# A spectral gate kernel: the inverse sequence step in 32x32 tiles, one joint last step for both branches

## The chip, the cores and the metric

The kernel runs on one core of one Trainium2 chip. The metric is device microseconds of one execution. Three runs of the kernel before gave 138.37, 138.78 and 139.69 us, with a median of 138.78. One more execution was profiled.

The engines are named as in the profile: PE is TensorE's matmul (PEld its weight load), DVE is VectorE, ACT is ScalarE, POOL is GpSimd and SP is SyncE, which issues most transfers. SPq and POOLq are the queues of transfers that SP and GpSimd issue.

## The reference

```python
B, S, D = 1, 2048, 1024; Df = D // 2 + 1

def ref(x, w_r, w_i):
    X = rfft2(x.astype(float32), axes=(-2, -1))
    X = X * (w_r + 1j * w_i)
    return irfft2(X, s=(S, D), axes=(-2, -1)).astype(bfloat16)

g = sigmoid((A_x * gate_w).sum(-1, keepdims=True))
out = g * ref(A_x, A_w_r, A_w_i) + (1 - g) * ref(A_x, B_w_r, B_w_i)
```

Both branches, A and B, transform the same x (2048 rows of 1024, bf16), so the forward transform is shared. Each branch multiplies it by its own complex weights (2048 x 513) and is transformed back. A gate g, one number per row, mixes the two results.

## The kernel before

A row's number is split as s = 16*p + n2, with p on the 128 partitions and n2 from 0 to 15; a frequency row is split as well. The transforms are matmuls with fixed matrices, in these steps. Every step leaves its result in PSUM, in units of 1,024 f32 per partition (two of the eight banks), and an **eviction** copies each unit to SBUF as bf16, on ACT or on DVE, whichever the plan gives it to (`ev`, line 469; on ACT it is recorded at line 479, on DVE at line 480). All matmuls are recorded at line 454 and all elementwise operations of two operands at line 457.

- **x and S1** (`xrows`, `stage_s1`): the 1,024 columns are folded into sums and differences (`fS`, `fT` on DVE), and 16 units of eight 256-column matmuls do the sequence transform over p. The result Z fills R3.
- **gate** (`gate_row`): matmuls on strips of 32 array columns, 512 wide, reduce Z with the folded gate weights.
- **D** (`stage_d`, 16 groups kg): the transform over d, eight matmuls of 256 columns each; its weights are slices of R3, so R3 is in use until the last D. Result Q.
- **S2** (`stage_s2`): the remaining 16-point step of the sequence transform, with full 128x128 matrices from SK. Result X in R4, shared by both branches. The frequency l=512 is kept apart (`x512`, `p512`, `v512`, `v512_row`).
- **PA, PB** (`prod`): the complex product with the weights of A and B. For two groups at a time DVE does a product of 2,048 elements (`mul`) and a sum of 1,024 (`sum`) for the real part and the same for the imaginary part: 32 products and 32 sums in all.
- **IA, IB** (`stage_i1`): per branch and group, eight matmuls of 256 columns do the inverse 16-point step. Result V, in R1 for A and in R5 for B.
- **EA, EB** (`stage_dinv`): per branch and n2, eight matmuls of 256 columns do the inverse over d: VA into R3, VB into a ring buffer. A Dinv needs all V of its own branch only, so A's can run while B's products are still made.
- **S** (`s1inv`): per n2, four matmuls of 512 columns do the inverse sequence step for both branches and add them in PSUM. The gate is folded into their matrices (`gmix`: RA, RB). DVE then unfolds the columns (`h0`, `h1`, `y0`, `y1`), and SP stores the rows.

The weights come in 28 transfers from SP (`wpart`), half of them in reversed rows of 513 elements (1,026 bytes). A's go to R5, B's to R2, which is free when the matrices F have been used by S1.

The order of the work is computed when the program is built. `Plan.run` is a list scheduler with estimated costs: among the operations that are ready on an engine it takes the one with the lowest rank and gives it an engine and PSUM or ring space. The rank is a line per kind of step from the table `ORDER` (line 18). Each engine then executes its own list in that fixed order, and waits on semaphores.

Of the kernel before, what the change touches and what calls it, by code (L numbers as in the profile page):

```python
# [15 lines left out]
KC = ((0, 4), (4, 8), (8, 16))  # L16
CELL = 512
ORDER = {"in": (0, 0), "x": (48.5, 5.31), "gate": (128.3, 6.12), "D": (35.3, 4.27), "S2": (2.5, 7.29),
         "PA": (46.6, 2.74), "IA": (49.9, 4.36), "x5": (67.7, 12), "row": (123.1, 12), "EA": (124.8, 11.5),
         "PB": (99.2, 5.5), "IB": (130, 4.9), "gm": (54.4, 5.49), "EB": (126.2, 10.71), "S": (130, 12),  # L20
         "U": (0.5, 2.73)}
DEPTH = ((0, 2), (2, 4), (4, 8), (8, 12), (12, 16))
# [8 lines left out]
def make_consts():  # L31
    C = {}
    pi2 = 2 * np.pi
    n1 = np.arange(128)[:, None, None]
    n2 = np.arange(16)[None, :, None]
    kord = np.arange(16)[:, None] + 32 * np.arange(4)[None, :]
    kord[0] = 0, 32, 16, 48
    kord = kord.reshape(-1)
    k1 = kord[None, None, :]
    a = pi2 * ((16 * n1 * k1 + n2 * k1) % 2048) / 2048.0  # L40
    F = np.zeros((128, 16, 64, 2))
    F[..., 0] = np.cos(a)
    F[..., 1] = -np.sin(a)
    F[:, :, 0, 1] = (-1.0) ** np.arange(128)[:, None]
    C["F"] = F.reshape(128, 2048)
    R = np.zeros((64, 2, 16, 128))
    at = a.transpose(2, 1, 0)
    R[:, 0] = np.cos(at) / 2048
    R[:, 1] = np.sin(at) / 2048
    R[0, 1] = ((-1.0) ** np.arange(128))[None, :] / 2048  # L50
    C["RM"] = R.reshape(128, 2048)

    m = np.arange(256)[None, :]
    DM = np.zeros((128, 4, 2, 256))
    for h in range(2):
        d = (h * 128 + np.arange(128))[:, None] + 0.5
        lev, lod = 2 * m, 2 * m + 1
        les = np.where(m == 0, 512, 2 * m)
        DM[:, 0, h] = np.cos(pi2 * lev * d / 1024)
        DM[:, 1, h] = -np.sin(pi2 * lod * d / 1024)  # L60
        DM[:, 2, h] = -np.sin(pi2 * les * d / 1024)
        DM[:, 3, h] = np.cos(pi2 * lod * d / 1024)
# [4 lines left out]
    for par in range(2):  # L67
        for h in range(2):
            l = (2 * (h * 128 + np.arange(128)) + par)[:, None]
            DI[:, par, h, 0] = np.where(l == 0, 1.0, 2.0) / 1024 * np.cos(pi2 * l * d / 1024)  # L70
            li = np.where(l == 0, 512, l)
            DI[:, par, h, 1] = -np.where(li == 512, 1.0, 2.0) / 1024 * np.sin(pi2 * li * d / 1024)
    C["DI"] = DI.reshape(128, 2048)

    S2 = np.zeros((2, 3, 128, 128))
    KI = np.zeros((2, 2, 128, 2, 16, 4, 2))
    for z in range(2):
        for pm in range(2):
            for k2 in range(16):
                for j in range(4):  # L80
                    po = pm * 64 + k2 * 4 + j
                    i, cj, spec = (3 - j if pm else j), pm == 1, False
                    if z == 1:
                        i, cj = ((0, 1, 0, 1), (2, 3, 3, 2))[pm][j], 32 * j + 16 * pm > 64
                        spec = i == 0
                    for q2 in range(16):
                        w = np.exp(-1j * pi2 * q2 * (k2 + cj) / 16)
                        if spec and j == 2:
                            w = w * np.exp(-1j * pi2 * q2 * 64 / 2048)
                        r0, r1 = q2 * 8 + i * 2, q2 * 8 + i * 2 + 1  # L90
                        wr, wi = w.real, w.imag
                        sg = -1.0 if cj else 1.0
                        if spec:
                            r = r1 if j == 2 else r0
                            S2[z, 0, r, po] = wr
                            S2[z, 1, r, po] = wi
                        else:
                            S2[z, 0, r0, po] = wr
                            S2[z, 0, r1, po] = -sg * wi
                            S2[z, 1, r0, po] = wi  # L100
                            S2[z, 1, r1, po] = sg * wr
                        cr, ci = wr, -wi
                        K = KI[z, :, po, :, q2, i, :]
                        if spec:
                            ri = 1 if j == 2 else 0
                            K[0, 0, ri], K[1, 0, ri] = cr, -ci
                            K[0, 1, ri], K[1, 1, ri] = ci, cr
                        else:
                            K[0, 0, 0], K[1, 0, 0] = cr, -ci
                            K[0, 0, 1], K[1, 0, 1] = -sg * ci, -sg * cr  # L110
                            K[0, 1, 0], K[1, 1, 0] = ci, cr
                            K[0, 1, 1], K[1, 1, 1] = sg * cr, -sg * ci
        S2[z, 2] = -S2[z, 1]
    C["SK"] = np.concatenate([S2.transpose(2, 0, 1, 3).reshape(128, 768),
                              KI.reshape(2, 2, 128, 256).transpose(2, 0, 1, 3).reshape(128, 1024)], 1)
    gs = np.full((64, 2), 8.0)
    gs[:, 1] = -8.0
    gs[0] = 4.0
    M = np.zeros((128, 64))
    M[:, :16] = gs.reshape(128, 1)  # L120
    M[::32, 16] = 1.0
    M[:16, 32:48] = np.eye(16)
# [135 lines left out]
class Plan:  # L258
# [28 lines left out]
    def run(self, keys):  # L287
# [18 lines left out]
        dma_free = 0.0  # L306
# [5 lines left out]
        def fit(t):  # L312
# [4 lines left out]
            if a == "ps":  # L317
                spots = range(0, 8, 2) if t.n == 2 else range(7, -1, -1)
            else:
                spots = range(len(c) - t.n + 1)  # L320
# [30 lines left out]
        while done < len(nodes):  # L351
            for e in ("sp", "pool", "pe", "act", "dve"):
                if free[e] > now + 1e-9:
                    continue
                for item in ready[e]:
# [7 lines left out]
                    if n.dma:  # L363
                        dma_free = max(dma_free, now + 1.3) + lat
                        n.end = dma_free + 0.9
# [39 lines left out]
def bass_gated_mix__spectral_gfnet__spectral_gfnet__prompt_kernel(  # L405
# [11 lines left out]
    def ap(t, off, dims, p0=0, np_=128):  # L417
# [4 lines left out]
    R3 = sb("R3", 16384)  # L422
    R4 = sb("R4", 16384)
# [3 lines left out]
    SK = sb("SK", 1792)  # L427
# [3 lines left out]
    NCELL = 26  # L431
    RING = sb("RING", NCELL * CELL)
    V6 = sb("V6", 256)
    X5 = sb("X5", 32)
    P5 = sb("P5", 192)
    V5 = sb("V5", 256)
# [5 lines left out]

    P = Plan({"ps": 8, "ring": NCELL, "late": 32},
             {"ps": ("ps", 4), "p1": ("ps", 8), "st": ("ring", 4), "q": ("ring", 3), "t": ("ring", 2),
              "pp": ("ring", 2), "g": ("ring", 1), "vb": ("ring", 4), "o": ("late", 3), "h": ("late", 2),
              "y": ("late", 3), "w": ("ring", 1)})
# [3 lines left out]
    WR = {0: R5, 1: R2}  # L450
    VR = {0: R1, 1: R5}
# [41 lines left out]

    def cload(eng, t, off, key, a, b, keys, **kw):
        dma("c_" + key, eng, lambda: [(ap(t, off, [[1, b - a]]).bitcast(dt.uint16), cst[key].ap()[:, a:b])],
            (b - a) * 256e-6, 400, [], keys, **kw)
# [16 lines left out]
    cload("sp", SK, 0, "SK", 0, 1792, ["SK"])  # L513

    def wpart(b, ci, pm, c):
# [3 lines left out]
        k0, k1 = KC[ci]  # L519
# [4 lines left out]
        def part(ka, kb, r0, step):  # L524
            o = [[n, kb - ka], [1, n]] if step < 0 else [[1, (kb - ka) * n]]
            i = [[step * n, kb - ka], [1, n]] if step < 0 else [[1, (kb - ka) * n]]
            prs.append((AP(T, 64 * pm * pt + c * NW + ka * NS, [[pt, 64]] + o),
                        AP(src.tensor, src.offset + r0 * n, [[32 * n, 64]] + i)))
        if pm == 0:
            part(k0, k1, k0, 1)  # L530
        else:
            if k0 == 0:
                part(0, 1, 16, 1)
# [265 lines left out]
    for n2 in range(16):  # L799
        stage_dinv(0, n2)  # L800
# [82 lines left out]
```

## Time and profile before

| what | us |
|---|---|
| median of three runs | 138.78 |
| span of the profiled execution, first to last instruction | 137.1 |
| DVE products, 32 of 2,048 elements | 38.1 |
| ACT evictions to R and RING, 105 of 1,024 elements | 74.6 + 32.4 |
| DVE evictions, 23 of 1,024 elements | 23.2 + 5.1 |
| PE matmuls of the inverse over d, 256 of 256 columns | 30.5 |
| PE matmuls of the inverse 16-point step, 256 of 256 columns | 31.0 |
| landing of a 513 KB weight transfer of B, from its issue | 18.5 to 20.2 |

The profiled execution's own whole time is not recorded apart from its span. The span runs from the first to the last instruction and lies 1.7 us below the median of the runs, which also hold what lies around the instructions. In the groups of the page the columns are line, engine, operation, output and input with their shapes and the count, then the busy time with the mean duration of one in ns, then the idle time of the engine just before, with what ended it. In the timeline rows the columns are start, length, engine and operation with the count; consecutive like operations are merged into one row. In the rows of ten engine slices each digit is the busy share of a 40th of the span (3.4 us).

### The profile page before, as it was taken

The numbers are of one execution on the slowest core, as the hardware profiler recorded it, in microseconds if no ns is written. First come the engines' busy times: TensorE is split into PE (matmuls) and PEld (weight loads), VectorE is DVE, ScalarE is ACT, GpSimd is POOL, SyncE is SP. The second block draws the span as 40 slices with busy tenths as digits, with TensorE's granted clock in tenths as the row PEclk, the third lists the DMA queues.
The fourth block names the chain that finished last, engine by engine and source line by source line (L and its number), as shares of the span: only waits on it lengthen the run. The fifth ranks groups of instructions, "written<-read, shape, count | busy, mean of one in ns | idle before, by whom it ended". The sixth has DMA issues, their size and how long they took to land.

```text
span 137.1 us, 2504 instructions
## 1 busy us (share of the span) xinstructions
PE 124.1 (91%) x1034; PEld 91.2 (67%) x1034; DVE 118.8 (87%) x159; ACT 112.7 (82%) x123; POOL 0.2 (0%) x4
## 2 busy tenths in 40 slices
PE   6859999999999949999977999999999999999930
PEld 2348886767778627766745888778887757666500
DVE  0399977389999679999999999999996889998992
ACT  6458886879989976999888799999787689898960
POOL 0000000000000000000000000000000000000000
PEclk9999999999999999999999999999999999999997
DMA  4999999999999999992000000000000021465254
GB/s 128 412 428 426 367 197 196 205 213 169 168 341 201 199 194 225 177 164 42 0 0 0 6 0 0 0 5 0 0 1 5 0 108 45 170 244 203 82 226 153
DMA packets 8269, 19.53 MB, mean 143 GB/s; under 512 B 961, under 2 KB 5057, under 8 KB 7618
## 3 DMA queue, kind: packets, MB, share of 16 engines
q1 hardware_dynamic: 8112, 19.36, 54.4%
q8 instruction: 8, 0.13, 0.5%
q10 hardware_dynamic: 146, 0.02, 0.1%
q14 instruction: 3, 0.02, 0.1%
HBM read 15.17 MB, written 4.19 MB: 141 GB/s over the span
## 4 chain that ended last, share of the span: by engine, by line
PE 53%; DMA 16%; DVE 15%; ACT 7%; SPq 3%; issue 3%; DVEq 0%
PE PS L454 53%; DMA R<-in_B_w_i_dram 13%; DVE RING L457 10%; ACT R L479 6%; DMA R<-in_A_x_dram 4%; SPq L485 3%; DVE R L480 3%; DVE R L457 1%; ACT RING L479 1%; DVE RING L480 1%; DVE P L457 0%; ACT V L479 0%; DVEq L215 0%; DVE X L480 0%
## 5 line engine op out<-in xcount | busy, mean ns | idle before, releaser
L479 ACT ACTIVATE R<-PS 128x1024 bf16<-128x1024 f32 x77 | 74.6, 1062 | 10.8 <-PE PS L454 10.6
L457 DVE TENSOR_TENSOR RING<-R 128x2048 bf16<-128x2048 bf16 (+1 forms) x48 | 48.3, 1046 | 6.8 <-DMA R<-in_A_x_dram 4.7
L479 ACT ACTIVATE RING<-PS 128x1024 bf16<-128x1024 f32 x28 | 32.4, 1180 | 4.0 <-PE PS L454 3.7
L454 PE MATMUL PS<-SK,RING 128*128 128x256 bf16 x256 | 31.0, 273 | 2.5 <-DVE R L480 1.9
L454 PE MATMUL PS<-DI,R 128*128 128x256 bf16 x256 | 30.5, 273 | 0.0
L454 PEld LDWEIGHTS PS<-SK,RING 128*128 128x128 bf16 x256 | 23.7, 98 | 7.5 <-DVE R L480 2.2
L454 PEld LDWEIGHTS PS<-DI,R 128*128 128x128 bf16 x256 | 24.7, 98 | 5.3 <-ACT R L479 0.2
L480 DVE CAST R<-PS 128x1024 bf16<-128x1024 f32 x19 | 23.2, 1223 | 4.4 <-PE PS L454 4.3
L457 DVE TENSOR_TENSOR R<-R 128x1024 bf16<-128x1024 bf16 (+1 forms) x36 | 21.3, 629 | 0.5
L457 DVE TENSOR_TENSOR RING<-RING 128x1024 bf16<-128x1024 bf16 x32 | 21.0, 689 | 0.1
L454 PE MATMUL PS<-RING,SK 128*128 128x511 bf16 (+1 forms) x96 | 16.9, 308 | 0.1
L454 PE MATMUL PS<-R,RING 128*128 128x256 bf16 x128 | 14.5, 273 | 2.0 <-DVE RING L457 1.4
L454 PE MATMUL PS<-DM,R 128*128 128x256 bf16 x128 | 16.1, 272 | 0.0
L454 PEld LDWEIGHTS PS<-R,RING 128*128 128x128 bf16 x128 | 12.3, 98 | 4.6 <-DVE RING L457 1.7
L454 PEld LDWEIGHTS PS<-DM,R 128*128 128x128 bf16 x128 | 11.6, 97 | 2.8 <-DVE R L480 0.4
L454 PEld LDWEIGHTS PS<-RING,SK 128*128 128x128 bf16 x96 | 7.7, 97 | 6.8 <-DVE RING L480 0.3
L454 PE MATMUL PS<-R,FM 128*128 128x512 bf16 x32 | 9.5, 379 | 0.4 <-ACT R L479 0.4
L454 PE MATMUL PS<-RING,DM 128*128 128x512 bf16 x32 | 9.5, 379 | 0.0
L480 DVE CAST RING<-PS 128x1024 bf16<-128x1024 f32 x4 | 5.1, 1264 | 3.0 <-PE PS L454 3.0
L454 PEld LDWEIGHTS PS<-RING,DM 128*128 128x128 bf16 x32 | 3.1, 98 | 3.8
L454 PE MATMUL PS<-RING 128*128 128x512 bf16 x10 | 4.4, 631 | 1.2 <-DVE RING L555 1.2
L454 PEld LDWEIGHTS PS<-R,FM 128*128 128x128 bf16 x32 | 3.0, 98 | 2.3 <-ACT R L479 0.9
(33 smaller groups left out, 27.3 us busy)
## 6 DMA issues: line engine op xcount, KB each, us to landing
out_dram<-R SPq DMA_DIRECT2D x7, 512.0 KB, 2.6
R<-in_A_x_dram SPq DMA_DIRECT2D x3, 1024.0 KB, 9.5
R<-in_A_w_r_dram SPq DMA_DIRECT2D x2, 513.0 KB, 19.0
R<-in_A_w_i_dram SPq DMA_DIRECT2D x2, 513.0 KB, 20.8
R<-in_B_w_r_dram SPq DMA_DIRECT2D x2, 513.0 KB, 18.5
R<-in_B_w_i_dram SPq DMA_DIRECT2D x2, 513.0 KB, 20.2
R<-in_A_x_dram SPq DMA_DIRECT2D x2, 512.0 KB, 4.6
R<-in_A_w_r_dram SPq DMA_DIRECT2D x3, 256.5 KB, 15.9
```

The source lines that it names most:

```text
L454: return lambda e: e.matmul(o, l, r, start=start, stop=stop, skip_group_check=True)
L457: return lambda e: e.tensor_tensor(out=o, in0=a, in1=b, op=op)
L479: return [lambda e: e.activation(o, i, ACT.Copy)]
L480: return [lambda e: e.tensor_copy(o, i)]
L485: lambda e: [lambda q, d=d, s=s: q.dma_start(d, s) for d, s in pairs()],
```

## The change

**The forward 16-point step and the inverse one in 32x32 tiles.** The frequency rows are ordered anew on the partitions (`kap`, `img` in `make_consts`), so that the 16-point steps act within blocks of 32 rows. S2 now has four groups sq. For each, four D (`j` = 0 to 3) give four Q, and two chunks of 32 matmuls of 512 columns follow, each with a 32x32 matrix at its own tile of the array. The Nyquist column l=512 is made by 64 one-column matmuls per group (S25) and one small eviction (X5) and then lies in the rows of X as the first or last of 513 columns; the old separate chain is gone.

**Products summed by TensorE.** `prod` does only the products, four per group sq and branch, each of 4 x 513 elements, into new areas (R2 for A, R5 for B). The sums are done in PSUM: `stage_i1` runs per group sq and part c a chunk of 64 matmuls of 512 columns in 32x32 tiles, four for each of sixteen tiles, into four banks, with two evictions of 1,024.

**Rows turned SBUF to SBUF.** V goes to ring buffers, and per branch and group four transfers of 256 KB (`turn`) move it so that the whole inverse sequence index lies on the partitions (TV: R1 for A, R2 for B). A transfer reads 128 partitions and writes 16 rows of 2 KB into each of 8 partitions. They are issued from GpSimd's queue, except that half of B's are issued by SP.

**One joint sequence step and one inverse over d.** For each n2, S1i is 16 matmuls of 128 columns (both branches added in PSUM, result G), and Di is eight matmuls of 256 columns. `stage_dinv` is gone. S1i reads the turned rows of both branches.

**Weights.** They come in 34 transfers per branch, each with 16 partitions. Those of A for j = 2 and 3 are issued from GpSimd's queue, after x rows 8 have landed. B's now go to R3, after Z has been read by all D and gate matmuls.

**Order.** Rank and, for many evictions, the engine are given per operation in two strings (`RANK`, `ENGS`) instead of the table `ORDER`. The scheduler keeps a separate transfer time line for each issuing queue. x comes in eight transfers instead of five.

```diff
-ORDER = {"in": (0, 0), "x": (48.5, 5.31), "gate": (128.3, 6.12), "D": (35.3, 4.27), "S2": (2.5, 7.29),
...
+WSPLIT = (((0, 4), (4, 16)), ((0, 8), (8, 16)))
+RANK = (
...
+DEPTH = ((0, 2), (2, 4), (4, 6), (6, 8), (8, 10), (10, 12), (12, 14), (14, 16))
...
-                        dma_free = max(dma_free, now + 1.3) + lat
+                        dma_free[e] = max(dma_free.get(e, 0.0), now + 1.3) + lat
...
-    WR = {0: R5, 1: R2}
-    VR = {0: R1, 1: R5}
+    WR = {0: R5, 1: R3}
+    TV = {0: R1, 1: R2}
+    PR = {0: R2, 1: R5}
...
+            prs.append((AP(T, (32 * j + odd) * pt + c * NW + ka * NS, [[2 * pt, 16]] + o),
+                        AP(src.tensor, src.offset + r0 * n, [[128 * n, 16]] + i)))
...
+        g = b == 0 and j > 1
+        dma("W%d%d" % (b, ci), "pool" if g else "sp", lambda: prs, (k1 - k0) * 0.0164, 205, [("x", 8)] if g else [], [("W", b, ci, j, odd, c)],
+            after=[("Z", m) for m in range(16)] if b else [], n=len(prs))
...
-                    f.append(mm(psl(t, o, [[1, 256]]), ap(R3, qq * 2048 + kg * 128, [[1, 128]]),
+                    f.append(mm(psl(t, o, [[1, 256]]), ap(R3, qq * 2048 + j * 512 + sq, [[4, 128]]),
...
-        ev("Q", 1024, lambda: (rg(q, 0, [[512, 2], [1, 2], [2, 256]]), psl(t, 0, [[512, 2], [256, 2], [1, 256]])),
-           [(t,)], [(q, 0, 2)], slow=True, alloc=[q])
+        ev("Q", 1024, lambda: (rg(q, 0, [[8, 2], [16, 64], [1, 8]]), psl(t, 0, [[512, 2], [8, 64], [1, 8]])),
+           [(t,)], [(q, 0, 2)])
...
+                            f.append(mm(psl(x5, (i * 2 + c) * 2 + u, [[1, 1]], 32 * j, 32), ap(SK, o, [[1, 32]]),
+                                        rg(qs[j], 1023 if u else 511, [[1, 1]]), True, True))
...
+                for m in range(2):
+                    for j in range(4):
+                        for i in range(4):
+                            w = z(i, j) + ((0, 2), (1, 0))[c][m] * 32
+                            f.append(mm(psl(t[i // 2], i % 2 * 512, [[1, 512]], 32 * j, 32), ap(SK, w, [[1, 32]], 32 * i, 32),
+                                        rg(qs[j], m * 512, [[16, 32], [1, 8], [8, 2]], 32 * i, 32), m == 0, m == 1))
...
-            P.add("sum", vt(1024), lambda e, t=t, c=c, op=op: [
...
+            w = ap(T, 2 * m * NS + o * NW, [[NS, 2], [(NW, -NW)[o], 2], [1, NS]])
+            P.add("mul", vt(4 * NS), lambda e, o=o, w=w: [tt(rp(b, p, (s0 * 4 + o * 2) * NS, [[4 * NS, 2], [NS, 2], [1, NS]]), x, w, ALU.mult)],
...
+                for pr in range(4):
+                    for j in range(4):
+                        for i in range(4):
+                            w = 192 + (192 if sq == i == j == 0 else 0) + (c * 3 + (0, 1, 2, 2)[pr]) * 32
+                            f.append(mm(psl(t[j // 2], j % 2 * 512, [[1, 512]], 32 * i, 32), ap(SK, w, [[1, 32]], 32 * j, 32),
+                                        rp(b, p, (i * 4 + pr) * NS + c, [[1, 512]], 32 * j, 32), pr == 0, pr == 3))
...
+        for j in (0, 2, 1, 3):
+            dma("turn", "sp" if b and j > 1 else "pool", lambda j=j: [(AP(TV[b], (32 * j + sq) * pit[id(TV[b])], [[4 * pit[id(TV[b])], 8], [1024, 16], [1, 1024]]),
+                                              rg(v[j // 2], j % 2 * 1024, [[1, 1024]]))], 0.262, 215,
...
+    allv = [("V", b, sq, j) for b in range(2) for sq in range(4) for j in range(4)]
...
+                        f.append(mm(psl(t, blk * 128, [[1, 128]]), ap(TV[b], off, [[2, 128]]), ap(rm, n2 * 128, [[1, 128]]), b == 0, b == 1))
...
+            pe("S1i", [128] * 16, fns, allv + [("RA", n2 // 4), ("RB", n2 // 4)], [(t,)], alloc=[t])
...
+            pe("Di", [256] * 8, fns, [(gt, 0, 2), "DI"], [(t,)], alloc=[t])
...
-    P.run(lambda n: ORDER[n.key[0]][0] + ORDER[n.key[0]][1] * n.key[1])
+    P.run(lambda n: int(RANK[2 * n.at:2 * n.at + 2], 36))
```

444 lines of the change are left out of this document (200 added, 244 removed), and 3 rows, old and new, of the table P.

## The prediction

> **What bounds the kernel now.** I read first the page's busy times and slices.
>
> ```profile
> span 137.1 us, 2504 instructions
> PE 124.1 (91%) x1034; PEld 91.2 (67%) x1034; DVE 118.8 (87%) x159; ACT 112.7 (82%) x123; POOL 0.2 (0%) x4
> PE   6859999999999949999977999999999999999930
> DVE  0399977389999679999999999999996889998992
> ACT  6458886879989976999888799999787689898960
> DMA  4999999999999999992000000000000021465254
> GB/s 128 412 428 426 367 197 196 205 213 169 168 341 201 199 194 225 177 164 42 0 0 0 6 0 0 0 5 0 0 1 5 0 108 45 170 244 203 82 226 153
> ```
>
> TensorE has hardly a gap from slice 3 to slice 38, and VectorE and ScalarE stand close behind it. DMA is full for the first 62 us and nearly idle from there to 110: x comes at 412 to 428 GB/s, then both weight sets at about 200. Then a table of busy time by stretch that I cut at the end of the sequence step (22.3), near the end of the first product's work (70), at the first joint output (100) and at the last matmul's end (131.5).
>
> ```profile
> 22.30:70.00 47.70, 45.76 (x397) 32.37 (x396) 42.42 (x50) 42.08 (x43) 0.00 (x0) 1.00 0.91 172
> 70.00:100.00 30.00, 28.26 (x275) 23.73 (x275) 29.95 (x41) 27.07 (x35) 0.00 (x0) 1.00 0.01 1
> 100.00:131.50 31.50, 31.04 (x221) 21.20 (x218) 28.27 (x41) 27.54 (x30) 0.00 (x0) 1.00 0.26 101
> 131.50:137.10 5.60, 0.00 (x0) 0.00 (x0) 2.96 (x8) 1.02 (x1) 0.00 (x0) 0.86 0.48 187
> ```
>
> The columns are PE, PEld, DVE, ACT, POOL, clock, DMA share, GB/s. PE fills every stretch; in 70 to 100 DVE is full too. So a gain needs all three engines relieved. The granted clock is 1.00 up to the tail. Prices come from the page's groups and from timeline rows:
>
> ```profile
> L479 ACT ACTIVATE R<-PS 128x1024 bf16<-128x1024 f32 x77 | 74.6, 1062 | 10.8 <-PE PS L454 10.6
> L457 DVE TENSOR_TENSOR RING<-RING 128x1024 bf16<-128x1024 bf16 x32 | 21.0, 689 | 0.1
> R<-V SPq DMA_DIRECT2D x2, 4.0 KB, 1.7
> 76.50 19.36 ACT L479 ACTIVATE R<-PS 128x1024 bf16<-128x1024 f32 x21 [0.77 <-PE PS L454]
> 68.50 0.61 PE L454 MATMUL PS<-R,G 128*32 128x512 bf16 x8
> 70.34 0.25 PE L454 MATMUL PS<-MS,FM 128*128 128x1 bf16 x4
> 70.77 0.42 PE L454 MATMUL PS<-MS,V 16*16 16x16 bf16 x8 [0.17 <-ACT V L479]
> 94.97 1.06 PE L454 MATMUL PS<-RM,ZG 128*128 128x128 bf16 x16
> 131.50 1.02 ACT L479 ACTIVATE R<-PS 128x1024 bf16<-128x1024 f32 x1 [0.21 <-PE PS L454]
> ```
>
> Durations overlap, so I price by spacing: an ACT eviction 19.36/21 = 0.92 us, a DVE eviction 1.14 (1.22 long; successors start 1.14 later), a 2,048-element product 1.14, a 256-column matmul 0.109 (92 in the full 10 us from 80), a 128-column one (1.06-0.22)/15 = 0.056. Eight gate matmuls of 512 columns on four 32-column strips take 0.61: 0.38 for one, 0.22 until the second four start, so four run side by side and start within some 4 ns of each other.
>
> **The change part by part.**
>
> *Removed.* The 32 sums: 21 us of DVE. Of 128 evictions of 1,024 elements 16 go: Z, Q, X and V stay at 16, 16, 16, 32, but VA+VB+o (48) become G+o (32). 14 Q evictions on ACT cost 1.32 instead of 1.02 (every second element is written); the new Q writes runs of eight, as V does already at 1.02, so I price it as V. On PE: S2 (64 x 0.215 = 13.8), I1 (256 x 0.109 = 27.9), both Dinv (27.9), S1i (13.8), and l=512's own chain with its two row DMAs.
>
> *Added on PE.* S1i is 256 matmuls of 128 columns, 256 x 0.056 = 14.3; one Di is 14.0. S2 is 256 and I1 1,024 matmuls of 32x32 with 512 columns. No row shows tiles in different rows running together. Bounds: all 16 at once, 0.216 per sixteen, gives 3.5 and 13.8; only the four columns at once, as the gate rows show, 0.864 per sixteen, gives 13.8 and 55. I take the first, since the gate rows show the 4 ns starts that it needs and neighbours in the new order lie in different tiles; both ends are kept. S25's 256 one-column matmuls lie between 4 ns (gate) and 35 ns (the 16x16 row: (0.42-0.17)/7), 1 to 9 us; I take 4, as two in a row share a tile. Each change of tiling costs about 0.1 (gate to D starts 0.32 after the last gate group, against 0.22): some 50 changes, 5 us. D's weights at step 4 are priced as I1's step 2, whose loads take 98 ns like unit-step ones; S2's moving operand at inner step 8 is unseen, at worst twice 3.5, and hidden. Between 22.3 and the joint step PE then has D 14 + S25 4 + S2 3.5 + I1 13.8 + gate and gm 3 + 5 = 43.
>
> [...]
>
> *Added on DVE.* Products have 2,052 elements instead of 2,048 in rows of 513. Weight rows of before start at odd offsets already and run at the 1.14 rate, so I add nothing; at worst an odd row length halves the rate, +1.14 x 32 = 36 us.
>
> *Added DMAs.* 32 turns of 256 KB, SBUF to SBUF, in 2 KB pieces: 24 from GpSimd's queue, 8 from SP's. GpSimd issues none before; its bound is an SP issue (0.55) below and an eviction-long 1.1 above, and only the last turns count. Landing: 1.7 (the 4 KB V row) at least, 2.6 (a 512 KB output) at most for one; I take 2.3 plus 0.6 of issue.
>
> [...]
>
> *Moved.* B's weights go to R3, so they wait until every D and gate matmul has read Z; before they followed the sequence step, and the last D runs at 61.8. Their 34 small issues queue on SP behind that wait with only output stores and turns behind them; 34 x 0.6 = 20 us of issue lies beside the transfer. A's weights are split between SP and GpSimd's queue, but the slices show about 200 GB/s at full DMA share for all weights, so splitting gives no more.
>
> *The sum, against the profiled 137.1.* (1) S1 is unchanged: its last matmul is at 22.3. (2) From there to the joint step VectorE and ScalarE have 64 evictions, 32 products (36.5), RA and RB 3.3, sigmoids and gate rows 5.0, X5 0.8. With a evictions on ACT, 0.92a+5.0 = 1.14(64-a)+40.6 gives a = 53 and 53.5 us each: more than PE's 43, so they are the bound. Start-up: four D (3.5), S25 and S2 (2), evictions, so the first product is near 30 as before, with only some eight Q evictions to do: 3 idle each. That ends at 78.8. (3) The joint step needs all rows of both products, a barrier that before has not: last I1 chunk 0.9, eviction 1.1, issue 0.6, landing 2.3: 5, so 83.8. (4) PE does S1i and Di, 28.3 plus 1.2 for the first G: 113.3 (VectorE and ScalarE have 32 evictions and 21 us of folds, 26 each, which fit). (5) The tail after the last matmul stays 5.6: 118.9. (6) Packing: before, PE's spacings between 9.6 and 131.5 add up to 115 of 122, 6% lost; 6% of stages 2 and 4 is 5, giving 123.9. The span lies 1.7 below the median of the runs (138.78), so **125.6**.
>
> Checked from the other side, B's weights: 32 evictions of Q and X, five by DVE before its products, 27 x 0.92 on ACT, put the last D near 47; 4.2 MB at 200 GB/s is 21; half of A's turns (4.2 MB at 428 GB/s, 10) shares the time, 5: 73. Eight products follow (9.1), then 5, 29.5, 5.6 and 1.7: 124. The two agree within 2, so either may be the one that ends last.
>
> **The rivals.**
>
> *B's weights land late (slower).* D spread between the products, as before (last one at 61.8), puts the landing at 61.8+21+5 = 88, and the time at 88+50.9 = 139. From a landing at 75 on, each us comes out at the end; from 88 the change loses. With the turns wholly inside it is 144; I take 142. For it: the wait is new, the slices show full DMA at 200 GB/s. Against: PE has 10 us of slack to run D early.
>
> *Issue binds the small tiles.* If each pair of load and matmul costs 29 ns, as in the row at 70.34 ((0.25-0.16)/3, all on one tile), the 256+1,024 pairs of S2 and I1 cost 37 instead of 17.3: PE's 43 becomes 63 against the others' 56.5, and 125.6 becomes 132. For it that row and the 16x16 one, against it the gate rows.
>
> *The tiles do not run together by rows,* so the change does not do what it says. S2 and I1 cost 69 instead of 17.3; PE has 95 in stage 2 against 56.5: 125.6+38.5 = 164, slower. Nothing for it but the lack of a row. Half-rate products (36 more on DVE, half of it passed to ACT as evictions: 144 to 162) share its chance.
>
> **How the numbers follow.** Forecast 0.55 (117 to 133), late weights 0.20, issue 0.12, serial tiles or half-rate products 0.10, 0.03 for better than 117 (early weights and full packing). The range 117 to 145 leaves out that 0.10, the 0.03 and a little of the late weights. Faster, by over 1% (below 137.4; less can't be told from no change): 0.55 + 0.10 of issue + 0.03 = 0.68. Within: 0.05 from the edges of issue and late weights. Slower: 0.10 + 0.17 = 0.27.
>
> **What would show it.** I1 chunks of 64 matmuls at 0.86 plus a switch (0.1): tiles together; 1.7 is issue, 3.5 serial. DVE and ACT at 95 each, PE below 100. Products at 1.22 long. The last D before 50, B's last weights near 74, the first joint matmul at 84 to 90, 29.5 from it to the last matmul, 5.6 after it. Wrong if products cost over 1.3, turns land later than 4, or a clock below 1.00 follows PE's idle time ahead of the joint step.

## The result, and the profile after

The changed kernel took 169.45 us (median of four runs, 167.99 to 171.67), the kernel before 138.64 beside it: a ratio of 1.2144, 95% interval 1.203 to 1.2257. The ratio leaves out the slowest of the four (171.67), which fell into a slower state. The change is slower; 125.6 was forecast. The profiled execution took 170.03, its span is 168.2.

The page of the changed kernel, its busy times and four of its slice rows (a slice is now 4.2 us):

```profile
span 168.2 us, 4991 instructions
PE 105.5 (63%) x2258; PEld 77.2 (46%) x2258; DVE 93.4 (56%) x116; ACT 97.9 (58%) x109; POOL 22.8 (14%) x44
...
PE   7898980099999975638620004761700599999950
...
PEclk9999999558999999996555555799585599999996
DMA  5999999992000056699999998078767000333635
GB/s 170 417 274 412 271 258 260 272 194 45 4 0 4 8 158 150 146 204 199 205 191 223 177 208 162 4 150 220 203 204 224 9 0 4 125 129 127 248 154 225
```

The work is as small as forecast: DVE 93 and ACT 98 against 95 each. Matmuls (PE) are at 105 of 168, where less than 100 was forecast, part of it at half clock. No engine is full any more. PE, at 9 nearly throughout before, has three holes: near 25 to 34 us, 85 to 103 and 122 to 132. The clock, 0.995 on average before, is 0.830, at 0.5 about those holes. DMA was nearly idle from 62 to 110 before; now it moves some 150 to 220 GB/s from 58 to 130, with one gap near 107, so it is busy in the holes too.

The same by stage: the wait ahead of D, D and S2, the rest up to the first product of B, from there to the joint step, the joint step (columns as in the table by stretch of before):

```profile
22.30:33.97 11.67, 2.49 (x37) 0.93 (x36) 0.69 (x1) 2.73 (x4) 0.00 (x0) 0.79 1.04 258
33.97:57.60 23.63, 23.63 (x408) 17.53 (x408) 14.04 (x16) 18.30 (x22) 0.00 (x0) 0.89 0.23 42
57.60:97.30 39.70, 18.06 (x771) 9.70 (x768) 17.15 (x20) 22.34 (x25) 9.48 (x16) 0.74 0.85 178
97.30:132.10 34.80, 11.88 (x513) 7.53 (x513) 20.77 (x18) 13.26 (x14) 4.74 (x8) 0.70 0.68 164
132.10:162.40 30.30, 29.95 (x384) 27.94 (x384) 23.44 (x33) 24.55 (x26) 0.00 (x0) 0.95 0.24 98
```

The joint step is as priced, and starts 48 us after the 83.8 of the forecast. From 57.6 to 132.1 the engines have work for 38 (DVE) and 36 us (ACT) in 74.5. What they wait for is in the groups and the list of transfers (the last figure there is the median from issue to landing):

```profile
L460 DVE TENSOR_TENSOR R<-R 128x2052 bf16<-128x2052 bf16 (+2 forms) x68 | 58.3, 908 | 22.9 <-DMA R<-in_B_w_r_dram 19.9
L457 PE MATMUL PS<-DM,R 128*128 128x256 bf16 (+1 forms) x256 | 34.2, 264 | 9.2 <-DMA DM<-c_DM 9.2
L457 PE MATMUL PS<-FM,R 128*128 128x128 bf16 x128 | 16.4, 229 | 10.4 <-DMA R<-RING 10.4
...
R<-RING POOLq DMA_DIRECT2D x24, 256.0 KB, 8.8
...
R<-in_B_w_r_dram SPq DMA_DIRECT2D x15, 128.2 KB, 9.9
...
DM<-c_DM SPq DMA_DIRECT2D x1, 512.0 KB, 21.7
```

Three arrivals, one for each hole. DM, the matrices of D, is issued at 12.2 among A's weights and lands at 33.9. B's products wait 19.9 us for B's weights: the last D ran at 57.6, the weights were issued from 57.9 to 94.0 and the last landed at 105.9. The joint step waits 10.4 us for the last turns, issued at 124.7 and 125.3 and landed at 132.1; over the 24 from GpSimd's queue the landing takes 8.8 in the median and up to 14.8. A fourth wait is in the timeline of PE, in I1 of A (the brackets hold the idle time before a row and what ended it; "issue" is time in which the profile shows nothing that was waited for):

```profile
71.63 1.14 PE L457 MATMUL PS<-R,SK 32*32 32x512 bf16 x64 [0.69 <-ACT R L482]
73.46 0.40 PE L457 MATMUL PS<-R,SK 32*32 32x512 bf16 x4 [0.69 <-ACT RING L482]
75.87 2.81 PE L457 MATMUL PS<-R,SK 32*32 32x512 bf16 x124 [2.01 <-issue]
79.11 0.61 PE L457 MATMUL PS<-R,SK 32*32 32x512 bf16 x4 [0.44 <-ACT RING L482]
81.47 3.63 PE L457 MATMUL PS<-R,SK 32*32 32x512 bf16 x124 [1.74 <-issue]
```

The first row is a chunk of 64 small matmuls in 1.14 us, so the sixteen tiles do run together. But twice PE stops after four matmuls and goes on 1.7 to 2.0 us later, after 128 pairs of load and matmul. During each stop the trace has a packet of 16 KB on the queue that the page lists as instruction (73.6 to 74.6 and 79.3 to 80.2).

### The profile page after: what moved, and what is told of

Read it like the earlier page. It is cut to its first block, busy times and chain, and to the rows that moved or that the text cites. A ratio compares the mean times of both kernels' runs of the same rounds, so it can differ in the third digit from the quotient of the medians.

```text
span 168.2 us, 4991 instructions
## 1 busy us (share of the span) xinstructions
PE 105.5 (63%) x2258; PEld 77.2 (46%) x2258; DVE 93.4 (56%) x116; ACT 97.9 (58%) x109; POOL 22.8 (14%) x44
## 4 chain that ended last, share of the span: by engine, by line
DMA 29%; SPq 25%; PE 25%; DVE 10%; ACT 5%; issue 3%; POOL 0%; DVEq 0%
SPq L488 25%; PE PS L457 25%; DMA DM<-c_DM 13%; DMA R<-RING 10%; DVE R L460 9%; DMA R<-in_B_w_r_dram 6%; ACT RING L482 5%; DVE RING L483 1%; ACT R L482 1%; POOL R L488 0%; DVEq L221 0%
## 5 line engine op out<-in xcount | busy, mean ns | idle before, releaser
L482 ACT ACTIVATE RING<-PS 128x1024 bf16<-128x1024 f32 x58 | 56.4, 1037 | 54.1 <-PE PS L457 52.5
L460 DVE TENSOR_TENSOR R<-R 128x2052 bf16<-128x2052 bf16 (+2 forms) x68 | 58.3, 908 | 22.9 <-DMA R<-in_B_w_r_dram 19.9
L457 PE MATMUL PS<-R,SK 32*32 32x512 bf16 x1024 | 24.2, 480 | 32.7 <-DVE R L460 21.9
L457 PE MATMUL PS<-DM,R 128*128 128x256 bf16 (+1 forms) x256 | 34.2, 264 | 9.2 <-DMA DM<-c_DM 9.2
L482 ACT ACTIVATE R<-PS 128x1024 bf16<-128x1024 f32 (+2 forms) x38 | 35.5, 987 | 7.7 <-PE PS L457 7.6
L457 PEld LDWEIGHTS PS<-R,SK 32*32 32x32 bf16 x1024 | 14.8, 92 | 42.8 <-DVE R L460 24.3
L457 PEld LDWEIGHTS PS<-DM,R 128*128 128x128 bf16 x256 | 27.3, 111 | 12.3 <-DMA DM<-c_DM 9.3
L457 PE MATMUL PS<-FM,R 128*128 128x128 bf16 x128 | 16.4, 229 | 10.4 <-DMA R<-RING 10.4
L483 DVE CAST R<-PS 128x1024 bf16<-128x1024 f32 (+2 forms) x14 | 14.8, 1071 | 3.6 <-PE PS L457 3.6
L457 PE MATMUL PS<-DI,RING 128*128 128x256 bf16 x128 | 15.2, 273 | 0.3 <-ACT RING L482 0.3
```

What stands on the lines that cost most here:

```text
L457: return lambda e: e.matmul(o, l, r, start=start, stop=stop, skip_group_check=True)
L460: return lambda e: e.tensor_tensor(out=o, in0=a, in1=b, op=op)
L482: return [lambda e: e.activation(o, i, ACT.Copy)]
L483: return [lambda e: e.tensor_copy(o, i)]
```

## The experiments

Three theories. **1**: late arrivals; DM, B's weights and the turns follow each other on one set of DMA engines. **2**: TensorE's small tiles, their instructions and the half clock. **3**: a turn is slow by its own form. "Joint" is the start of the joint step (132.1 in the changed kernel). The edits change `P.order`, the finished order, behind `P.run`, except where other lines are shown. Times are of one run each with a profile, except in the one run whose interval is given; the kernel before took 138.7 to 140.4 beside them. The changed kernel's own four runs lie 3.7 us apart, so a difference of one or two us between single runs says little.

### The order of the loads

```diff
+    early = [n for n in P.order if n.name in ("c_DM", "c_SK")]
+    rest = [n for n in P.order if n not in early]
+    k = 1 + max(i for i, n in enumerate(rest) if n.name == "x" and n.eng == "sp")
+    P.order = rest[:k] + early + rest[k:]
```

> Only the loads of DM and SK move: they are issued by SP right after the last x load instead of among A's weights; every engine's order is otherwise that of the changed kernel. Theory 1 (a chain of late arrivals, because the weights on two queues share one set of DMA engines): D starts at 23 to 25 instead of 33.97, the last D ends near 47 instead of 57.8, B's weights are issued from there, and the whole time falls by about the same 10 us, to 157 to 163. Theory 2 (small tiles at the pace of issue hold TensorE): D starts earlier, but the time stays within 4 of 170. Theory 3 (the turns set the end by their own slowness): at most 5 of the 10 arrive at the end, 165 to 168.

164.4 us, between the ranges of theories 1 and 3 and outside that of theory 2. D starts at 25.8 instead of 34.0, and the last one runs at 52.2; 5.6 of the 8.2 us come out at the end, against the profiled run's 170.0. Next, with it, B's weights in two halves, the first one first:

```diff
+    wb = iter(sorted((n for n in P.order if n.name in ("W10", "W11")), key=lambda n: n.name))
+    P.order = [next(wb) if n.name in ("W10", "W11") else n for n in P.order]
```

> The load of the D matrices goes ahead of A's weights (as in the first experiment, 164.4 us), and of B's weights the first half (frequency rows k2 0 to 7, all that the first four product groups need) is issued before the second half; nothing is left out. Theory 1 (a chain of late arrivals): the first product of B starts near 75 instead of 88, the second half lands near 90 while the first half's products run, the joint step starts at 115 to 120, time 153 to 159. Rival, theory 3 (the turns set the pace behind the products, whatever their start): the first product comes early, but the ring stays full of rows waiting to be turned, the joint step stays within 4 us of the first experiment's 125.8, time 160 to 165. Theory 2 (issue of small matmuls): no change against 164.4, since no matmul is taken away.

161.3 us, joint 123.3. B's first product starts at 75.2 as theory 1 had it, but that of the second half only at 99.1: the gain of 13 us at the front is 2.5 at the joint step. Time and joint step are in the ranges of theory 3. The second half's product did wait for its weights, the last of which landed at 99.0. Then with both, half of B's weights from GpSimd's queue:

```diff
+    for n in P.order:
+        if n.name in ("W10", "W11") and n.writes[0][4]:
+            n.eng = "pool"
```

> As the run with the D matrices early and B's first half first (161.3 us), and half of B's weights (the reversed rows) issued from GpSimd's queue beside SyncE's; nothing is left out. If SyncE's issue of about 0.8 to 1.0 us for each of 34 transfers holds B's weights back: all issued by 70 instead of 81, second half's products by 92 instead of 99, time 153 to 158. If the DMA engines themselves are full: products at 99 as before, 160 to 165 (the turns on GpSimd's queue are pushed back too).

160.7 us, in the range for full DMA engines; the 0.6 us is within the spread. The issue of the weights still went on to 81.8, and the second half's first product came at 96.9. But its weights had landed at 90.5, and in the page of this run the products' largest wait is for TensorE, and TensorE's is no longer for data:

```profile
L460 DVE TENSOR_TENSOR R<-R 128x2052 bf16<-128x2052 bf16 (+2 forms) x68 | 58.3, 908 | 21.5 <-PE PS L457 11.2
L457 PE MATMUL PS<-R,SK 32*32 32x512 bf16 x1024 | 27.0, 501 | 25.6 <-issue 16.6
```

Two stops of PE ahead of small matmuls last 5.0 and 5.7 us here, while the DMA share is at 1.0. A product of the second half needs the area that I1 of the first half reads, so it comes after these stops. Where all of B's weights were issued by 70 (further down, from GpSimd's queue alone) they had landed at 83.4 and that product still came at 91.8. There it waited for TensorE, TensorE 9.9 us for an eviction of ScalarE, and ScalarE 7.5 us for turns that had to free the ring.

### What each transfer costs

```diff
+    P.order = [n for n in P.order if n.name not in ("W10", "W11")]
+    for n in P.order:
+        n.reads = [k for k in n.reads if not (k[0] == "W" and k[1] == 1)]
-            w = ap(T, 2 * m * NS + o * NW, [[NS, 2], [(NW, -NW)[o], 2], [1, NS]])
+            w = ap(T, (0 if b else 2 * m * NS) + o * NW, [[NS, 2], [(NW, -NW)[o], 2], [1, NS]])
```

> B's weights are not loaded; B's products read what lies in R3 instead and wait for nothing there. Theory 1: VectorE's wait of 19.9 us for B's weights goes and A's turns have the DMA engines to themselves, so B's products run from about 77; the joint step starts near 103 instead of 132.1 and the time is 138 to 147. Theory 2: TensorE's small tiles still hold it, over 158. Theory 3: both branches' turns, 8.4 MB at the some 200 GB/s of the changed kernel's last turns, take 42 us from the first one at 66, so 145 to 150.

157.9 us, above the ranges of theories 1 and 3 and at the bound of theory 2. B's products start at 78.0 instead of 97.3 and the joint step still only at 119.7: 19 us at the front are 12 at the joint step, and something stands behind the weights. With that run alone it could be the turns or TensorE.

```diff
+    P.order = [n for n in P.order if not (n.name == "turn" and n.key[0] == "IB")]
+    for n in P.order:
+        n.reads = [k for k in n.reads if not (k[0] == "V" and k[1] == 1)]
```

> B's sixteen turns are left out, and the joint step reads R2 as it is, without waiting for them. Theory 1 with the turns as its last link: B's products run without a break from 97.4 to about 116 and the joint step starts near 118 instead of 132.1: 154 to 158. If TensorE's own pace in B's inverse 16-point step holds the end (theory 2), the joint step starts at 126 or later: 163 or more.

153.5 us, half a microsecond below theory 1's range, joint 116.4: 16.5 us for B's turns alone. With the first edit of all (DM early), no weights of B and, by the edit above without its condition on the branch, no turns at all:

> The load of the D matrices goes ahead of A's weights, B's weights are not loaded (B's products read what lies there) and none of the 32 turns is made. Left are all matmuls, products and evictions, with x, A's weights and the constants as transfers. Theory 1 alone: the stage falls back to the forecast's sum of VectorE and ScalarE, joint step at 84 to 90, time 121 to 128. Theory 2 beside it (pairs of load and small matmul wait for their instructions, and the clock falls after idle time): joint step at 96 to 104, time 133 to 141.

128.5 us, joint 91.4, at the edge of theory 1's range. Its stage from the last D to the joint step:

```profile
50.50:91.40 40.90, 26.22 (x1281) 15.27 (x1280) 36.46 (x36) 34.21 (x38) 0.00 (x0) 0.89 0.01 4
```

VectorE is busy 36.5 of 40.9, as the forecast's sum wanted it. So what the change does to the engines is worth some 10 us (138.6 to 128.5) when none of these transfers is made, and the transfers left out here, with the place of DM, cost 41.

### The form of a turn

All turns from GpSimd's queue, in place of 24 there and 8 on SyncE's:

```diff
+    for n in P.order:
+        if n.name == "turn":
+            n.eng = "pool"
```

> B's eight turns that SP issues go to GpSimd's queue, at the same places of the order. If a turn runs on half of the DMA engines only, and SP's always on the same half, all sixteen from one queue spread better: B's turns take some 16 us instead of 24 and the time is 161 to 166. If the turns are slow because GpSimd's queue is (median landing 8.8 us), it gets worse: 172 to 180. If the turns do not matter: 168 to 171.

172.9 us, at the lower end of the range for a slow queue, but only 1.2 above the highest run of the changed kernel, so it decides little. Then the turns as straight copies, on the queues of the changed kernel:

```diff
-            dma("turn", "sp" if b and j > 1 else "pool", lambda j=j: [(AP(TV[b], (32 * j + sq) * pit[id(TV[b])], [[4 * pit[id(TV[b])], 8], [1024, 16], [1, 1024]]),
+            dma("turn", "sp" if b and j > 1 else "pool", lambda j=j: [(ap(TV[b], (4 * sq + j) * 1024, [[1, 1024]]),
```

> The 32 turns become straight copies: the same source, queue, 256 KB, 128 pieces of 2 KB and waits, but each piece is written to its own partition instead of sixteen pieces to each of eight partitions (so the rows are not turned, and the sequence step reads other numbers). If the write into few partitions is what makes a turn slow, the median landing falls from 8.8 us to below 5 and the time to 156 to 163. If it is SBUF to SBUF, or GpSimd's queue, that is slow, landing stays at 8 to 9.5 and the time at 168 to 172.

154.7 us, faster than expected if the form is the cost, and about as fast as without B's turns. SyncE's copies, when the weights had landed, took 3.7 us; those on GpSimd's queue, beside the weights, still 8.5. With bytes, pieces and waits the same, the form of the turn costs some 15 us. Which part of the form, the next two tell for turns from ScalarE's queue. Turns from ScalarE (`n.eng = "act"` in the edit above), and with it copies of 128 partitions for A and 119 for B:

```diff
+            dma("turn", "sp" if b and j > 1 else "pool", lambda j=j: [(ap(TV[b], (4 * sq + j) * 1024, [[1, 1024]], 0, 119 if b else 128),
+                                              rg(v[j // 2], j % 2 * 1024, [[1, 1024]], 0, 119 if b else 128))]
```

> All 32 turns are issued by ScalarE in place of GpSimd (24) and SyncE (8); nothing is left out. In the trace of the changed kernel 2.1 MB of turns from GpSimd's queue cost 9 us of all 16 DMA engines, 2.1 MB from SyncE's 4 us (difference to the run without B's turns). If the queue is what makes turns slow: landing below 6, joint step 5 to 10 us earlier, time 158 to 166. If it is the shape of the turn or SBUF to SBUF: landing stays near 8.8, time 167 to 172. ScalarE's waits for VectorE's evictions and its issue time (32 times up to 0.6) work against: 170 to 178 if they decide.

> Straight copies in place of the turns, all issued by ScalarE: A's 16 of 128 partitions, B's 16 of 119 partitions (7 percent fewer bytes; the rows are not turned, and the last nine partitions of B's are left as they are). This tells apart two reasons for the slowness of a turn. [...] If it is the write into few partitions, B's copies run as fast as A's: share above 0.7 or landing near the straight copies' 3.7 us, joint step by 118, time 150 to 157.

166.5 us, between the two ranges, and 161.8, above the 150 to 157 for the write into few partitions; the other reason is that fewer DMA engines carry such a copy. In the table by stretch, 104 to 112 us, when B's weights have landed and turns or copies are queued, first the run with turns, then that with copies of 119 partitions (the last two columns are DMA share and GB/s):

```profile
104.00:112.00 8.00, 4.23 (x128) 2.40 (x128) 4.11 (x4) 4.75 (x6) 0.00 (x0) 0.50 0.53 201
```

```profile
104.00:112.00 8.00, 4.80 (x176) 2.50 (x144) 4.31 (x4) 4.40 (x5) 0.00 (x0) 0.60 0.46 159
```

A turn has 8 destination partitions, and the share of 0.53 is the time of 8.5 of 16 DMA engines; with 119 partitions 0.46 is that of 7.4, though each piece has its own partition. So from this queue it is the count of engines at work, not the write into few partitions: some 22 to 24 GB/s for each. The packets say the same: ScalarE's queue has 4,498 in the run with turns and 146 where it issues none, so 136 for a turn, 128 pieces and 8 more. A straight copy of 128 partitions has 144 (128 and 16, from the 4,754 of the run with copies from ScalarE further down), which leaves 126 for one of 119 (119 and 7, from 4,466). What sets the count no run tells.

For GpSimd's queue, which issues 24 of the 32 turns in the changed kernel, this does not explain the slowness. In the run without B's weights, with turns from that queue alone under way:

```profile
85.00:90.00 5.00, 4.01 (x131) 2.56 (x131) 2.64 (x3) 2.52 (x4) 2.12 (x4) 0.50 1.02 203
```

The rate is the same, 203 GB/s, but the DMA share is 1.02, all 16 engines. For the same 8.4 MB, 24 turns and A's weights, the queue takes 25.0% of 155.8 us here, 39 us of all engines, and 19.4% of 152.9, 30 us, with straight copies for the turns, beside B's weights. So sixteen engines alone do not make a turn faster; whether its write into few partitions has a limit of its own near 200 GB/s stays open.

### Both together, and what else is late

The early DM, the halves, half of the weights from GpSimd's queue and all turns from ScalarE, then the same with straight copies:

> As the run before it, and all turns issued by ScalarE; nothing is left out. On ScalarE's queue turns took half the DMA share that they take on GpSimd's at the same 200 GB/s, which leaves the rest to the weights. Theory: second half's products by 90, joint step at 103 to 110, time 140 to 148. If both are bound by the same memory path, no better than the run before it.

> As the run before it (D matrices early, B's first half first and on two queues, turns from ScalarE: 158.8 us), with straight copies of 128 partitions in place of the turns, so that all 16 DMA engines carry them (the rows are not turned). The account to be closed: order of the loads and half the DMA engines together are what the change lost. After the last D at 52, 4.2 MB of weights at 200 GB/s (21 us) and 8.4 MB of copies at some 400 (21) share the engines: no end of B's copies before 95. Theory: second half's products by 82, joint step at 95 to 104, time 133 to 142, about level with the kernel before. If something else holds B's rows back (the ring of buffers, instruction fetch, half clock), joint step at 108 or later, time above 146.

158.8 us and 153.4 (ratio to the kernel before 1.0991, 1.0862 to 1.112). The theory's ranges failed in both, joint at 120.5 and 113.7 instead of 103 to 110 and 95 to 104; the second lies where something else was to hold B's rows back (108 or later, above 146). In the second, rows of PE ended by ScalarE's evictions stand between B's chunks, and ScalarE issues transfers between them, at some 0.6 each. So all turns went to SyncE and all of B's weights to GpSimd's queue, where no engine that evicts is held up:

```diff
+    for n in P.order:
+        if n.name in ("W10", "W11"):
+            n.eng = "pool"
+        if n.name == "turn":
+            n.eng = "sp"
```

> D matrices early, B's first half first, all of B's weights issued from GpSimd's queue and all 32 turns by SyncE, so that no engine that evicts issues transfers; nothing is left out. In the run before (copies from ScalarE, 153.4) ScalarE spent some 0.6 us on each of 32 issues between its evictions. If that held B's rows back there and the eight DMA engines of the turns hold them back here: 8.4 MB of turns at 200 GB/s are 42 us from the first turn near 61, so the joint step starts at 105 to 113, time 143 to 151. If fetched instructions and the half clock hold TensorE back whatever issues the transfers: joint step at 114 or later, time 152 or more.

> The run before it with straight copies of 128 partitions in place of the turns (the rows are not turned), so all 16 DMA engines carry them. If ScalarE's issues were what held the run of 153.4 back: joint step at 96 to 104, time 134 to 142, 8 or more below the run with turns. If TensorE's instruction fetch and half clock do: joint step at 107 to 114, within 4 of the run with turns.

158.7 us (joint 119.8) with turns, 145.0 (106.2) with copies. Moving the issues off ScalarE, and with it all weights to GpSimd's queue, gave the turns nothing; the copies gained 8.4 us by it. The run with turns lies in the range for instructions and half clock, that with copies between its two ranges: something is left beside the half set of engines. In the copies' run PE shows it:

```profile
65.66 0.40 PE L457 MATMUL PS<-R,SK 32*32 32x512 bf16 x4 [0.70 <-ACT RING L482]
68.89 3.35 PE L457 MATMUL PS<-R,SK 32*32 32x512 bf16 x124 [2.83 <-issue]
72.97 0.40 PE L457 MATMUL PS<-R,SK 32*32 32x512 bf16 x4 [0.74 <-ACT RING L482]
77.68 3.63 PE L457 MATMUL PS<-R,SK 32*32 32x512 bf16 x124 [4.31 <-issue]
```

The stops after 128 pairs last 2.8 and 4.3 us here, with the DMA share at 1.03 from 60 to 76. With weights and turns both away the longest such stop was 1.5, and beside the weights alone 1.8. So two of the four product terms were left out of I1:

```diff
-                for pr in range(4):
+                for pr in (0, 3):
```

> The run before it with two of the four product terms in the inverse 16-point step (512 of its 1,024 small matmuls left out, their instructions too). If TensorE's small matmuls, their instruction fetch or the half clock are late last, the joint step comes 6 to 12 us earlier than there. If transfers and evictions are, it moves by less than 2.

140.7 us, joint 101.0: 5.2 earlier with half of I1's matmuls, between the two expectations. Theory 2 holds for a part. And for the run with turns, every second eviction of B's rows by VectorE:

```diff
+    vb = [n for n in P.order if n.name == "V" and n.key[0] == "IB"]
+    for n in vb[1::2]:
+        n.eng = "dve"
```

> The run with turns from SyncE, and every second eviction of B's rows given to VectorE, which waits there, in place of ScalarE; nothing is left out. If ScalarE's evictions (four in a row for each group, 0.95 each) are late last behind the second half's products: 3 to 6 us faster than that run. If the turns are: within 2.

158.8 us, no change: the evictions are not what is late there. Last, on the same base (158.7), the turns without B's weights and the weights without turns:

> The run with all turns issued by SyncE (158.7 us, joint step at 119.8) without B's weights (not loaded; B's products read what lies there). With neither (128.5 us) the joint step started at 91.4. If transfers after the last D pass one after the other at 200 GB/s: 8.4 MB of turns take 42 us from the first at 59, so the joint step starts at 102 to 106, time 139 to 144. If turns are hidden once the weights are gone: joint step at 94 to 97, time 131 to 135.

> The same run (158.7 us) with B's weights and without the 32 turns (the sequence step reads what lies there). 4.2 MB from the last D at 52 land by 74 to 78, and the products of B can follow the fourth of A's groups without a wait from 70 on: joint step at 92 to 97, time 129 to 134, so that weights alone cost at most 5 us over neither and weights and turns together 28. If B's weights alone are late: joint step at 103 or later.

146.5 us, a little above the range for transfers one after the other, and 132.4, in the range for weights that cost little. The weights alone, issued from 52.0 to 68.9, had all landed at 76.0. With the 128.5 of neither:

| after the last D | time | joint |
|---|---|---|
| neither | 128.5 | 91.4 |
| B's weights alone | 132.4 | 94.4 |
| turns alone | 146.5 | 107.3 |
| both | 158.7 | 119.8 |
| both, copies for turns | 145.0 | 106.2 |

Three stretches of the run with turns alone, where nothing else is loaded:

```profile
80.00:88.00 8.00, 5.23 (x239) 3.58 (x240) 6.85 (x7) 4.76 (x5) 0.00 (x0) 0.79 0.53 200
88.00:96.00 8.00, 4.23 (x173) 2.52 (x144) 2.39 (x3) 5.54 (x6) 0.00 (x0) 0.79 0.54 201
96.00:104.00 8.00, 0.00 (x0) 0.00 (x0) 0.85 (x1) 0.28 (x1) 0.00 (x0) 0.64 0.52 201
```

From 72 to 104 turns move at 200 GB/s at half the share without a break, and in the last stretch TensorE has nothing left to do but wait for them: they set the pace. Weights alone cost 4 us, the turns 18, and both 30, more than their sum. An explanation that fits, but that no run isolates, is that the weights need the eight engines too that carry the turns: with both under way, from 60 to 76, the engines moved 196 to 208 GB/s at a share near 1. After the last D at 52, 12.6 MB at 200 GB/s are 63 us, to 115; the joint step starts at 119.8.

## Why the prediction was wrong, point by point

*Step 1, S1 unchanged: its end right, what follows wrong.* S1's last matmul ended at 22.8 against 22.3. But the sum let D start there, and D waited for DM until 34.0. The order comes from `RANK`, and the load's place in it was not worked out; putting it ahead of A's weights gains 5.6 us.

*Step 2, VectorE and ScalarE as the bound: their work right, the stage wrong.* Products take 1.22 us, and a chunk of I1 1.14 where 0.96 was priced. A chunk of S2, with half as many matmuls, takes 1.19, so a matmul there costs about double, as its worst case had it; its operand at inner step 8 may be why, but the order of the tiles differs too. With the transfers gone, that bound nearly holds: 128.5, where the forecast less the turn's 2.9 is 122.7. So packing (step 6, 5 us) was some 6 too small, with D's start at 24.3 instead of 22.3 in it.

*Step 3, the barrier of 5, is the step that failed.* It priced the landing of a turn at 2.3 and held that only the last turns count. The last ones took 7 us to land, but the larger error is that this sum put the others at nothing. The 32 turns are a stream of 8.4 MB, which at 200 GB/s takes 42 us, and it fills the ring of buffers on the way, so that evictions wait for turns (5.9 us ahead of the last two of B). Left alone with their transfers, the turns cost 18 us (128.5 to 146.5), with B's weights beside them 26 (132.4 to 158.7). At half of the x loads' 428 GB/s they would be 39; that turns move at about half of that, no run of before showed.

*Steps 4 and 5 right:* 30.3 from the first joint matmul to the end of the last against 29.5, and 5.8 after it against 5.6.

*The cross-check failed in each of its terms ahead of the joint step:* last D 57.6 for 47; the weights' 21 plus 5 for half of A's turns, taken at 428 GB/s, became 48 (57.9 to 105.9). Without turns the weights took 24 (52.0 to 76.0), so the 21 was close and the turns' share of 5 was not. Agreement of the two sums proved nothing, since both held the same small price for the turns. The scheduler of the diff makes the same error by its code: it counts the transfers of each issuing queue on a time line of their own, as if each queue had DMA engines to itself.

*The rivals.* "B's weights land late" named the direction and the wait, but with 88 for the landing. By its own price, one us at the end for each from 75 on, 105.9 gives 125.6 + 30.9 = 156.5; the other 13 lie behind the weights, with B's turns, which no rival had. "Issue binds the small tiles" was wrong in size of a pair (1.14/64 = 18 ns, not 29), right in that TensorE stops for more than data: after 128 pairs, for 1.7 to 2.0 us in I1 of A, with a packet on the instruction queue during the stop, which reads as a wait for instructions. Tiles run together by rows (the 1.14 for 64), and products in rows of 513 take 1.22 us, so the half rate of the worst case was not shown. Of what was to prove the forecast wrong, two came: turns landing later than 4 (8.8 in the median), and a clock below 1.00 (0.70 from 97.3 to the joint step).

What stays open: how the last 15 us between copies (joint 106.2) and neither (91.4) divide between full DMA, the stops after 128 pairs and the half clock, of which half of I1 moves 5; and what holds turns from GpSimd's queue at 203 GB/s with all engines busy.

## What to carry to other kernels

Before a change that replaces arithmetic by transfers is priced, add up all bytes that must land before its barrier, each at the rate measured for its form and queue (here some 200 GB/s for a turn, 294 for straight copies in a stretch without weights), against one set of DMA engines whatever queue issues them (half of B's weights on a second queue gained 0.6 us); a landing time of one transfer says nothing of thirty-two. And in a kernel whose order is a table, look up where each load stands in it: one 512 KB constant behind a set of weights held every engine for 9 us.

## What the runs showed of the hardware

- A copy into 8 partitions (a turn) moved 201 GB/s at a DMA share of 0.53, one of 119 partitions 159 at 0.46, both from ScalarE's queue; straight copies of 128 from SyncE's moved 294 at 0.79 (92 to 100 us, when B's weights had landed). From GpSimd's queue the copy into 8 partitions moved 203 at 1.02.
- The changed kernel's page counts 18 packets, 0.29 MB, on a DMA queue of the kind instruction (16 KB each in the trace), and where PE stops in its small matmuls the stops lie 128 pairs of load and matmul apart. Two chunks of small matmuls, 128 pairs, take as little as 2.2 us. The stops of TensorE at these places were up to 1.5 us with weights and turns both away, 1.7 to 2.0 in the changed kernel's I1 of A, 2.8 and 4.3 with straight copies beside the weights, 5.0 and 5.7 with half of the weights on GpSimd's queue beside the turns. The DMA share alone does not set them: it was between 0.84 and 1.11 during all of the last three kinds of stop, and beside the weights alone, at 1.06, they were 1.2 and 1.8.
- After such holes the granted clock was 0.50, also while TensorE worked. The table by stretch and the timeline of PE in the run with B's weights alone:

```profile
76.00:84.00 8.00, 5.24 (x179) 3.40 (x180) 5.06 (x5) 5.52 (x7) 0.00 (x0) 0.50 0.01 2
```

```profile
66.14 1.15 PE L457 MATMUL PS<-R,SK 32*32 32x512 bf16 x64 [0.69 <-ACT RING L482]
...
78.30 3.95 PE L457 MATMUL PS<-R,SK 32*32 32x512 bf16 x128 [2.30 <-ACT RING L482]
82.71 3.95 PE L457 MATMUL PS<-R,SK 32*32 32x512 bf16 x128 [0.47 <-ACT RING L482]
...
91.60 1.40 PE L457 MATMUL PS<-R,SK 32*32 32x512 bf16 x64 [0.51 <-DVE R L460]
```

A chunk of 64 takes 1.15 at full clock and half of 3.95 at half clock, with the DMA engines idle (share 0.01): the work after the holes was slower as well. Two rows of 3.95 us with 0.47 between them did not bring the full clock back: it was 0.50 from 76 to 84 and 0.56 from 84 to 92. After a third, from 87.1 to 91.1, it was 1.00 (92 to 96), while small tiles went on (the last row above). What brought it back, and whether the gaps held it down, no run tells.
